# State products in pairs, a third one-pass block, one prefix scan and a new order, in a fused Mamba-2 and SiLU kernel on one core

## The chip, the core and the metric

The kernel runs on one NeuronCore of a Trainium2 chip. The core has five engines that run side by side, each with its own queue in program order: PE (matrix products; the loading of its stationary operand is shown apart, as PEld), DVE (vector operations), ACT (activations and copies), POOL (GpSimd) and SP, which here only issues DMAs. The metric is device time in microseconds, the median of several executions. One more execution was profiled; all durations of instructions below come from that one.

## What is computed

For each of 4 x 8 (batch, head) a state-space recurrence over 768 steps, in chunks, and behind it a SiLU layer over all tokens:

```python
# x (4,8,768,32)  a (4,8,768)  B, C (4,8,768,16), fp32
log_a = log(clip(a, 1e-6, 1));  cum = cumsum(log_a) within the chunk
y   = ((C @ B.T) * exp(cum_i - cum_j) * causal) @ x  +  (C @ state) * exp(cum)
state = exp(sum(log_a)) * state + (B * exp(cum_last - cum)).T @ x
# tokens (3072, 256) = y with the heads side by side
h = X @ w_in            # 256 -> 2048
out = (h * sigmoid(h)) @ w_out   # 2048 -> 256
```

All inputs and outputs are fp32.

## The kernel before

**Tiling.** The sequence work is cut into 12 units of 256 tokens of one batch (three units to a batch, numbered u = 0 to 11), each with four chunks of 64 steps. Two units make a pair (P = 0 to 5, 512 tokens), and the SiLU layer runs by pairs: W_in in 8 blocks of 256 columns (numbers 0 to 7), W_out in 8 blocks (8 to 15).

**Order.** Nothing is scheduled by a compiler. One text, SCHEDULE, lists some 1,300 tokens; each token calls one function, which issues its instructions. The order of tokens is the order of every engine's queue. SLOTS lists, in the order in which tiles are asked for, the buffer that each gets (pools of 49 tiles of 512 floats a partition, "s2k"; 12 of 1024, "r4k"; 7 of 1024, "raw"; 3 PSUM banks, "hp"). Two PSUM tiles of two banks each, ga and gb, serve the small products of the units and the first products of the SiLU layer in turn; one more bank, o_ps, serves the rest. Waits between engines follow from the tiles.

**Tokens of a unit u** (small products, with the array cut into tiles of 32 or 64 rows): `La` loads the decay of unit u, broadcast to all partitions, from a DRAM copy az; `E` (line 511) scans it to the matrix of decays; `Lp` loads the same values of a from a second DRAM copy, ac, and `P` (line 483) scans them to prefix products PFX; `Ln`, `Lt`, `Lx` load B, C and x; `T` transposes (line 524), `ce` scales C by head parity (545), `B` scales B by the decay (519, POOL), `C` scales C by PFX (550, POOL for most units). On PE: `gd` (function f_D0, line 570) makes each chunk's contribution to the state, `g0` (f_G0, 584) makes C.B for all chunks, `Y` (f_Y, 634 and 643) makes the output from the state and from the matrix M. On DVE `M` (599) multiplies g0's result by the decays, `S` (614) runs the state from chunk to chunk. ACT copies: `b` (593), `SM` (622), `y` (671), `xh` (678). `xh` and `x` split the unit's output into three parts, XK.

**Tokens of the SiLU layer.** fp32 products on PE take several passes per product; a product of fp32r operands takes one. So most of the layer is done with operands that are split into three parts, h, l and d, with one product for each part. `lw` loads a weight block, `u`, `v`, `w` and `W` turn it into a form whose parts can be cut exactly, `H` (line 322, ACT) cuts h, `lD` (326, DVE) makes l = h + w, `dD` (330, DVE) makes d = Z*h + l. For pair P and block i: `a` (line 799) does the h and l products of W_in, eight of 512 columns, `ax` (810, ACT) rescales in PSUM, `d` (799) adds four d products, `dg` (820, ACT) applies SiLU, `h`, `l`, `e` (826, 650, 836) split the result, and `q` (781) multiplies one half block by one half of W_out, three products. For pair 0, W_out is applied in full precision (`n1`, line 760), and W_in in full precision (`s`, line 696, one unit at a time, with `si` as SiLU) for blocks 0 to 5, and with `a` and `d` for blocks 6 and 7. `z` issues products with a zero tile whose result nobody reads (438: 512 columns; 440: six of 64 columns).

**a.** At the start i_a loads a for the first two units (`ia`), which PE transposes (`AT`); `ir` loads all of a, `AA,0` and `AA,1` clip it on POOL, `AD,4` writes az and `AD,0` to `AD,3` write ac, by POOL's DMA queue.

**Dead code that matters later.** Line 333 on has two functions that no token of before calls: w_part (an ACT copy of h, or of Z*h, into the tile for l or d) and w_more (a DMA issued by POOL that adds another tile to it), as `Wl`, `Wd` and `Wm`, `We`.

Of the kernel before, what the change touches and what calls it, by code (L numbers as in the profile page):

```python
# [30 lines left out]
w,9,2 dD,7 n1,1,1 ax,0,7 w,6,1 lw,10 s,0,2 w,6,2 v,15 u,10 w,15,2 d,0,7 si,0,2 W,11 lw,12 H,11 v,12 Lx,2,0,0 Lt,3,1,3,0
T,3,1 n1,0,0 v,13 n1,1,0 n1,6,1 La,2,1,0 dg,0,7 tq,2 La,2,0,0 E,2,1 W,15 w,10,0 n1,7,1 n1,15,1 n1,14,1 E,2,0 B,2 Lp,2,0
P,2 u,12 w,12,0 w,12,1 ce,2,0 Lt,3,0,2,0 g0,2 M,2,1 Lt,4,1,3,0 v,10 La,3,1,0 Lx,2,1,0 gd,2 n1,6,0 b,2,1 M,2,0 lw,14
n1,14,0 W,9 W,6 n1,2,0 w,13,2 Lt,3,0,1,0 n1,3,1 Lt,4,1,1,0 ce,3,1 H,5 Lx,3,0,0 H,9 b,2,0 S,2,0 S,2,1 S,2,2 ce,3,0 H,1
SM,2,1 n1,7,0 n1,15,0 C,2 u,14 SM,2,0 Y,2 La,3,0,0 E,3,0 W,13 v,14 si,1,4 w,10,2 y,2,0 Lt,4,1,2,0 H,6 E,3,1 Lt,3,0,3,0
T,3,0 Ln,3,0,1,0 Lx,3,1,0 Lp,3,0 P,3 n1,2,1 Ln,3,0,0,0 B,3 gd,3 w,12,2 W,12 Lt,4,0,0,0 lD,6 y,2,1 xh,2 g0,3 M,3,0 b,3,1
C,3 b,3,0 n1,10,1 n1,3,0 a,0,6 w,10,1 W,10 Lt,4,0,3,0 lD,0 S,3,0 S,3,1 M,3,1 dD,6 n1,11,0 H,13 S,3,2 Lp,4,0 w,14,0
Lt,4,1,0,0 w,14,1 Lx,4,1,0 ax,0,6 n1,10,0 x,2,1 H,15 SM,3,0 d,0,6 w,14,2 H,8 n1,5,0 La,4,1,0 n1,9,0 x,2,0 lD,5 La,4,0,0
E,4,0 Ln,4,0,1,0 dg,0,6 SM,3,1 Y,3 y,3,1 y,3,0 xh,3 lD,3 W,14 H,14 n1,13,0 n1,12,0 T,4,1 ce,4,0 n1,5,1 lD,9 n1,9,1 x,3,0
a,1,0 ax,1,0 n1,13,1 dD,5 Lt,4,0,2,0 x,3,1 n1,8,1 Lt,4,0,1,0 T,4,0 lD,1 ce,4,1 S,3,3 dD,0 d,1,0 P,4 C,4 n1,11,1 E,4,1  # L40
dg,1,0 lD,8 n1,12,1 dD,8 H,10 Lt,5,0,1,0 g0,4 Lx,4,0,0 Ln,4,0,0,0 B,4 H,4 gd,4 b,4,0 dD,1 M,4,1 b,4,1 S,4,0 S,4,1 S,4,2
SM,4,1 n1,4,0 M,4,0 Lt,5,1,1,0 SM,4,0 lD,4 Lt,5,1,0,0 lD,2 S,4,3 dD,2 h,1,0 dD,3 l,1,0 e,1,0 n1,8,0 n1,4,1 Vn,0 lD,10
Y,4 y,4,0 n1,0,1 y,4,1 a,1,1 xh,4 dD,10 H,12 lD,12 Vn,1 Lt,5,0,0,0 ax,1,1 a,1,2 ax,1,2 Lt,5,1,2,0 d,1,1 dg,1,1
Ln,5,0,0,0 Lt,5,1,3,0 T,5,1 La,5,1,0 o,0,0,2 q,1,0,0,1 La,6,1,0 ce,5,1 La,5,0,0 Ln,5,0,1,0 d,1,2 dg,1,2 h,1,2 ce,5,0
Lt,6,1,2,0 a,1,3 ax,1,3 q,1,0,1,1 a,1,4 ax,1,4 d,1,3 dg,1,3 Lp,5,0 q,1,0,1,0 E,5,1 E,5,0 B,5 o,0,1,2 lD,13 AD,2 lD,11
dD,4 Lx,5,0,0 l,1,2 e,1,2 d,1,4 dg,1,4 q,1,2,1,0 q,1,0,0,0 Lt,5,0,2,0 Lt,5,0,3,0 T,5,0 lD,15 dD,12 g0,5 x,4,1 Lx,5,1,0
Ln,6,0,0,0 gd,5 P,5 M,5,1 h,1,4 h,1,1 l,1,4 q,1,2,0,1 a,1,5 q,1,2,1,1 e,1,4 q,1,4,0,1 q,1,2,0,0 La,6,0,0 b,5,0 S,5,0
AD,3 Lt,6,1,1,0 q,1,4,0,0 b,5,1 ax,1,5 d,1,5 Ln,6,0,1,0 S,5,1 S,5,2 SM,5,0 M,5,0 SM,5,1 dD,13 Lt,6,1,3,0 x,4,0 q,1,4,1,1
q,1,4,1,0 C,5 dD,9 dg,1,5 h,1,5 Y,5 Lp,6,0 y,5,1 l,1,1 y,5,0 e,1,1 q,1,1,1,1 a,1,7 O,0,0,2,1,0 l,1,5 Lt,6,1,0,0
q,1,1,0,1 q,1,1,0,0 ax,1,7 e,1,5 d,1,7 Lt,6,0,0,0 xh,5 q,1,5,1,0 E,6,1 Lx,6,0,0 q,1,5,0,1 dg,1,7 Lt,6,0,3,0 T,6,1 ce,6,1  # L50
P,6 x,5,0 ce,6,0 Lt,6,0,2,0 Lt,6,0,1,0 T,6,0 q,1,5,0,0 E,6,0 h,1,7 C,6 g0,6 B,6 M,6,1 Lx,6,1,0 gd,6 b,6,0 Lt,7,1,2,0
h,1,3 q,1,1,1,0 S,6,0 M,6,0 dD,15 b,6,1 q,1,5,1,1 a,2,1 ax,2,1 S,6,1 S,6,2 SM,6,1 a,1,6 ax,1,6 l,1,7 e,1,7 q,1,7,0,0
q,1,7,0,1 d,1,6 dD,11 x,5,1 Lt,7,0,1,0 q,1,7,1,1 q,1,7,1,0 dg,1,6 d,2,1 l,1,3 e,1,3 lD,14 q,1,3,0,0 h,1,6 Lt,7,1,3,0
q,1,3,0,1 SM,6,0 l,1,6 dg,2,1 h,2,1 Y,6 La,7,1,0 y,6,0 e,1,6 Lt,7,1,0,0 Lx,7,1,0 S,6,3 Lt,7,1,1,0 T,7,1 ce,7,0 y,6,1
# [72 lines left out]
def kernel(  # L127
# [231 lines left out]
    def pz01(u):  # L359
        return held(f"pz{u}", [128, 4, Q + 1])  # L360
# [527 lines left out]
```

## Time and profile before

| | us |
|---|---|
| median of 3 runs | 333.38 (331.79 to 334.20) |
| the profiled execution: time | 333.58 |
| its span, first to last instruction | 331.8 |

| engine | busy us of 331.8 |
|---|---|
| PE | 321.9 |
| PE's weight loads | 244.0 |
| DVE | 250.8 |
| ACT | 204.9 |
| POOL | 48.6 |

The profile tells, for each engine, when each instruction began and ended, and what released it when its engine had been idle. Groups of instructions are named by the line of the kernel, the engine, the operation and the tiles (output <- inputs), with count, busy time, mean duration in ns, and the idle time just before them. The chain of work goes back from the last instruction, at each step to what released it. Durations of matmuls overlap, so the pace is read from the chain, not from the mean. 26.64 MB are moved by DMA, 80 GB/s on the mean; the ten loads of `pz` from ac carry 130 KB each.

### The profile page before, as it was taken

What the parts mean: (1) busy time and instruction counts of PE and PEld (TensorE: products, weight loads), DVE (VectorE), ACT (ScalarE), POOL (GpSimd) and SP (SyncE); (2) the same over time, 40 slices, a digit from 0 to 9 for tenths busy, and PEclk for the clock granted to TensorE, in tenths of its full rate; (3) what the DMA queues carried; (4) which work ended last, traced back from release to release, by engine and by line L of the source; (5) the groups of instructions that cost most, each with busy time, mean ns of one, the idle gap of its engine ahead of it and who ended that gap; (6) DMA issues with size and microseconds to landing.
All of it is one profiled execution on the core that took longest, in us unless ns stands there. A gap on an engine that the chain in (4) does not pass through costs nothing.

```text
span 331.8 us, 7522 instructions
## 1 busy us (share of the span) xinstructions
PE 321.9 (97%) x3078; PEld 244.0 (74%) x3078; DVE 250.8 (76%) x350; ACT 204.9 (62%) x309; POOL 48.6 (15%) x64
## 2 busy tenths in 40 slices
PE   6799999999999999999999999999999999999995
PEld 2478874455587878787887887877888787878884
DVE  4887899999999989698966678956486845453663
ACT  4669787644777565766566677726576367674811
POOL 2435565341111010010010100010000000000000
PEclk9769999999999999999999999999999999999999
DMA  5999478342253311245227241250003300031002
GB/s 173 218 276 256 173 202 197 63 94 34 69 117 69 73 48 21 53 109 123 29 38 152 73 89 30 38 111 2 2 9 70 58 2 0 2 54 18 2 0 63
DMA packets 93522, 26.64 MB, mean 80 GB/s; under 512 B 79840, under 2 KB 86752, under 8 KB 93488
## 3 DMA queue, kind: packets, MB, share of 16 engines
q1 hardware_dynamic: 90960, 25.71, 34.3%
q10 hardware_dynamic: 2352, 0.26, 0.6%
q8 instruction: 24, 0.39, 0.5%
q0 software_dynamic: 176, 0.20, 0.3%
q14 instruction: 10, 0.08, 0.1%
HBM read 22.81 MB, written 3.34 MB: 79 GB/s over the span
## 4 chain that ended last, share of the span: by engine, by line
PE 78%; DVE 12%; DMA 4%; ACT 2%; issue 1%; SPq 1%; POOL 1%; DVEq 0%; POOLq 0%
PE hp L781 27%; PE ga L799 15%; PE gb L799 15%; PE o_ps L781 5%; PE hp L696 5%; PE hp L760 3%; DVE ab L511 3%; PE ga L634 2%; PE ga L584 2%; PE ga L643 1%; DVE ab L599 1%; DMA bn<-in_B_dram 1%; DVE s2k L330 1%; DVE s2k L326 1%; DMA tbc<-in_C_dram 1%
## 5 line engine op out<-in xcount | busy, mean ns | idle before, releaser
L781 PE MATMUL hp<-r4k,s2k 128*128 128x512 f32 x400 | 109.5, 394 | 0.0
L781 PEld LDWEIGHTS hp<-r4k,s2k 128*128 128x128 f32 x400 | 74.0, 188 | 16.4 <-issue 0.5
L650 DVE SCALAR_TENSOR_TENSOR r4k<-r4k,r4k 128x1024 fp32r<-128x1024 f32 (+1 forms) x42 | 50.4, 1199 | 36.6 <-ACT r4k L826 28.9
L799 PE MATMUL ga<-raw,s2k 128*128 128x512 f32 x240 | 62.1, 394 | 0.0
L799 PE MATMUL gb<-raw,s2k 128*128 128x512 f32 x240 | 62.0, 393 | 0.1
L799 PEld LDWEIGHTS gb<-raw,s2k 128*128 128x128 f32 x240 | 44.5, 188 | 11.6 <-ACT gb L810 1.2
L799 PEld LDWEIGHTS ga<-raw,s2k 128*128 128x128 f32 x240 | 44.6, 188 | 11.3 <-ACT ga L810 1.2
L836 DVE SCALAR_TENSOR_TENSOR r4k<-r4k,r4k 128x1024 fp32r<-128x1024 f32 x40 | 48.7, 1222 | 4.9 <-PE o_ps L781 1.5
L826 ACT ACTIVATE r4k<-r4k 128x1024 fp32r<-128x1024 f32 x40 | 41.9, 1057 | 2.0 <-PE hp L781 0.5
L810 ACT ACTIVATE ga<-ga 128x1024 f32<-128x1024 f32 x21 | 21.2, 1009 | 20.5 <-PE ga L799 20.5
L820 ACT ACTIVATE r4k<-gb 128x1024 f32<-128x1024 f32 x21 | 21.5, 1025 | 15.6 <-PE gb L799 15.4
L810 ACT ACTIVATE gb<-gb 128x1024 f32<-128x1024 f32 x21 | 21.2, 1008 | 15.6 <-PE gb L799 15.6
L820 ACT ACTIVATE r4k<-ga 128x1024 f32<-128x1024 f32 x21 | 21.5, 1024 | 15.0 <-PE ga L799 13.8
L781 PE MATMUL o_ps<-r4k,s2k 128*128 128x512 f32 x80 | 30.7, 390 | 0.0
L760 PE MATMUL hp<-r4k,s2k 128*128 128x512 f32 x64 | 30.1, 602 | 0.0
L318 POOL TENSOR_TENSOR s2k<-s2k,s2k 128x512 uint32<-128x512 uint32 (+1 forms) x19 | 24.1, 1280 | 22.6 <-DVE s2k L310 13.7
L519 POOL TENSOR_TENSOR BT<-bn,ab 128x256 f32<-128x256 f32 x10 | 7.3, 730 | 120.3 <-DVE ab L511 87.5
L511 DVE TENSOR_TENSOR_SCAN ab<-ab,diag 128x512 f32<-128x512 f32 x20 | 24.8, 1246 | 0.0
L696 PE MATMUL hp<-r4k,s2k 128*128 128x256 f32 x96 | 22.9, 395 | 0.0
L696 PEld LDWEIGHTS hp<-r4k,s2k 128*128 128x128 f32 x96 | 18.7, 199 | 3.4 <-issue 0.4
L760 PEld LDWEIGHTS hp<-r4k,s2k 128*128 128x128 f32 x64 | 11.6, 189 | 10.8 <-issue 9.3
L599 DVE TENSOR_TENSOR ab<-gb,ab 128x512 f32<-128x512 f32 x12 | 8.2, 686 | 12.3 <-PE gb L584 7.4
(123 smaller groups left out, 390.9 us busy)
## 6 DMA issues: line engine op xcount, KB each, us to landing
ab<-az SPq DMA_DIRECT2D x20, 256.0 KB, 4.2
raw<-in_moe_w_in_dram SPq DMA_DIRECT2D x8, 512.0 KB, 4.1
raw<-in_moe_w_out_dram SPq DMA_DIRECT2D x8, 512.0 KB
out_dram<-r4k SPq DMA_DIRECT2D x44, 64.0 KB, 2.9
xt<-in_x_dram SPq DMA_DIRECT2D x20, 128.0 KB, 2.6
pz<-ac SPq DMA_DIRECT2D x10, 130.0 KB
bn<-in_B_dram SPq DMA_DIRECT2D x20, 64.0 KB, 3.6
tbc<-in_C_dram SPq DMA_DIRECT2D x36, 32.0 KB, 3.7
```

Of the source, the lines that this page charges most:

```text
L318: nc.gpsimd.tensor_tensor(out=u[:, :, fs], in0=u[:, :, fs], in1=v[:, :, fs], op=ALU.add)
L511: nc.vector.tensor_tensor_scan(out=o, data0=src, data1=diag.rearrange("p h t -> p (h t)"), initial=0.0, op0=ALU.mult, op1=ALU.add)
L599: nc.vector.tensor_tensor(out=o, in0=DP[u][w][:, :, 0:256].rearrange("p g (k x) -> p k g x", k=2), in1=o, op=ALU.mult)
L650: nc.vector.scalar_tensor_tensor(out=l, in0=f32(h), scalar=BACK, in1=y, op0=ALU.mult, op1=ALU.add)
L696: nc.tensor.matmul(out=hp[:, i], lhsT=WT[j][:, kc, 128 * i:128 * i + 128], rhs=XM()[:, 2 * kc:2 * kc + 2, u], start=(kc == 0), stop=(kc == ...
L760: nc.tensor.matmul(out=NP[m], lhsT=WT[8 + f // 2][:, f % 2, 128 * m:128 * m + 128], rhs=GT[0, f // 2][:, f % 2], start=(n == 1), stop=(n = ...
L781: nc.tensor.matmul(out=ACC[P, c], lhsT=WK[8 + i, p][:, k, 128 * m:128 * m + 128], rhs={"h": HT, "l": LT, "d": DT}[p][P, i][:, k], start=(n ...
L799: nc.tensor.matmul(out=o, lhsT=WK[j, q][:, kc, 128 * i:128 * i + 128], rhs=xs[:, 2 * kc:2 * kc + 2], start=(start and q == "h" and kc == 0 ...
L810: nc.scalar.activation(t, t, AF.Copy, scale=1.0 + Z)
L820: nc.scalar.activation(g, t, AF.Silu, scale=BACK)
L826: nc.scalar.activation(t, GT[G, i], AF.Copy, scale=-LESS * Z)
L836: nc.vector.scalar_tensor_tensor(out=DT[G, i], in0=f32(HT[G, i]), scalar=-1.0, in1=f32(LT[G, i]), op0=ALU.mult, op1=ALU.subtract)
```

## The change

It changes four things.

1. **Units 6 to 11 in pairs.** The tokens `Y,6` to `Y,11` become `YY,6`, `YY,8` and `YY,10`: f_Y does the state products of both units, then the products with M of both, into the two halves of ga and gb. So that the second unit of a pair can wait with its operands, its BT, CW and SM lie in a tile of the "raw" pool instead of the shared one, and its gd goes to other columns of ga. Before the first YY the order of gd and g0 is: gd,6 g0,6; gd,7; g0,7. Then gd,8; gd,9 g0,8; g0,9. Then g0,10 gd,11 gd,10; g0,11. (A semicolon stands where other products lie between.)
2. **Block 5 of pair 0** goes from `s` (two units) to `a,0,5`, `ax,0,5`, `d,0,5`, `dg,0,5`. `H,5`, `lD,5` and `dD,5` come earlier.
3. **One scan.** The ten `P` scans go. `AP` scans acp, all chunks and heads at once (48 partitions x 520), between `AA,1` and `AD,0`; so ac holds prefix products, and `Lp` loads them into PFX, two buffers in turn.
4. **A new order** of all tokens and slots. In it, W_out blocks 10 to 15 get l, and blocks 12 to 15 also d, by `Wl`/`Wm` and `Wd`/`We` instead of `lD` and `dD`. The large `z` go from 11 to 10, the groups of six small ones from 6 to 17; nine large and all 17 groups stand before the first `s`.

```diff
-cp cI c1 lw,4 ci z,1 z,1 z,1 z,1 ia,0 ct v,4 ia,1 z,1 z,1 z,0,6 z,1 cd ip,0,0 z,1 co u,4 ca A AT AU as,1,0 lw,0 ir,0 z,1
+ch ia,0 ca co cI cp ci z,0,6 z,0,6 z,0,6 ia,1 Lt,0,1,3,0 z,1 z,1 Ln,0,0,1,1 z,0,6 z,1 Ln,0,0,0,1 z,0,6 ip,0,0 c1 cd A AT
...
+q,2,1,1,1 h,2,2 g0,7 SM,6,0 q,2,1,0,1 q,2,0,1,1 M,7,1 q,2,0,0,1 M,7,0 SM,7,0 SM,7,1 YY,6 y,6,1 Lp,8,0 La,8,0,0 l,2,2
...
+PAIRS = (6, 8, 10)
...
-    one = const.tile([128, 4, Q + 1], FP32, name="one")
...
     def load_pz(u, q):
-        PZ[u] = keep("pz", [128, 4, Q + 1], loads)
+        PFX[u] = keep("pfx", [128, 4, Q + 1], loads2, u % 2)
...
-    def f_P(u):
-        PFX[u] = keep("pfx", [128, 4, Q + 1], loads)
-        nc.vector.tensor_tensor_scan(out=PFX[u].rearrange("p c t -> p (c t)"),
-                                     data0=PZ[u].rearrange("p c t -> p (c t)"),
-                                     data1=one.rearrange("p c t -> p (c t)"), initial=0.0,
+    def f_AP():
+        t = acp().rearrange("p h t -> p (h t)")
+        nc.vector.tensor_tensor_scan(out=t, data0=t, data1=one().rearrange("p h t -> p (h t)"), initial=0.0,
                                      op0=ALU.mult, op1=ALU.add)
...
+    def second(u, i):
+        return u - 1 in PAIRS and held(f"bc{u}", [128, 4, UT], key="raw")[:, i]
...
+        if not early and u - 1 in PAIRS:
+            d = [DP[u][0][:, c, 384:512] for c in range(2)]
...
-    def f_Y(u):
+    def f_Y(u, n=1):
         y = gy()
+        for v in range(u, u + n):
+            first = v % UPB == 0
+            st, cw, c0 = SM[v], CW[v], 128 * (v - u)
...
+        for v in range(u, u + n):
+            m, xc, c0 = M[v].rearrange("p k g (e t) -> p k (g e) t", e=2), xt[v], 128 * (v - u)
...
+            YO[v] = y, c0
```

The two functions that the new order calls and the old one did not:

```python
    def w_part(n, p):
        t = WK[n, p] = small(f"{p}{n}", [128, 2, WF], FR)
        nc.scalar.activation(t, f32(WK[n, "h"]), AF.Copy, scale=1.0 if p == "l" else Z)

    def w_more(n, p):
        other = WT[n] if p == "l" else f32(WK[n, "l"])
        nc.gpsimd.dma_start(out=f32(WK[n, p]).rearrange("p k f -> p (k f)"),
                            in_=other.rearrange("p k f -> p (k f)"), accum_op=ALU.add)
```

More of the change, by code (lines that the diff above doesn't have):

```diff
@@ L212, in f32 @@
         return t.bitcast(FP32)
-    bn, tbc, xt, E, M, BT, BH, CT, CE, CW, PFX, ST, SM, DP, BX, YS, PZ = ({} for _ in range(17))
+    bn, tbc, xt, E, M, BT, BH, CT, CE, CW, PFX, ST, SM, DP, BX, YS = ({} for _ in range(16))
     def at(u):
@@ L357, in acp, with one @@
         return held("acp", [NCH, H, Q + 1], key="r4k")
+    def one():
+        return held("one", [NCH, H, Q + 1], key="r4k")
     def pz01(u):
@@ L421, in c_one @@
     def c_one():
-        nc.gpsimd.memset(one, 0.0)
-        nc.gpsimd.memset(one[:, :, 0:1], 1.0)
+        nc.gpsimd.memset(one(), 0.0)
+        nc.gpsimd.memset(one()[:, :, 0:1], 1.0)
     def c_acp():
@@ L547, in f_C @@
     def f_C(u):
-        CW[u] = keep("cw", [128, UT], sc)
+        CW[u] = second(u, 1) if u - 1 in PAIRS else keep("cw", [128, UT], sc)
         engine = nc.vector if 0 < u < UPB else nc.gpsimd
@@ L619, in f_SM @@
         if u not in SM:
-            SM[u] = keep("sm", [128, 4, 64], sc)
+            if u - 1 in PAIRS:
+                SM[u] = second(u, 2).rearrange("p (t x) -> p t x", t=4)
+            else:
+                SM[u] = keep("sm", [128, 4, 64], sc)
         if True:
@@ new lines, in f_Y @@
+        for v in range(u, u + n):
+            first = v % UPB == 0
+            st, cw, c0 = SM[v], CW[v], 128 * (v - u)
+            for t in range(1 if first else 0, 4):
+                k, c = divmod(t, 2)
+                for g in range(4):
+                    w, q = divmod(g, 2)
+                    nc.tensor.matmul(out=y[w][64 * q:64 * q + 64, c, c0 + 64 * k:c0 + 64 * k + 64],
+                                     lhsT=st[32 * g:32 * g + 32, t], rhs=cw[32 * g:32 * g + 32, Q * t:Q * t + Q],
+                                     start=(v == u and (k == 0 or (first and t == 2))), stop=False,
+                                     tile_position=(32 * g, 64 * q), skip_group_check=True)
```

215 lines of the change are left out of this document (105 added, 110 removed), and 6 rows, old and new, of the table SLOTS.

## The prediction

> **What bounds the kernel now.** I read the page first: span, busy shares, the chain.
>
> ```profile
> span 331.8 us, 7522 instructions
> PE 321.9 (97%) x3078; PEld 244.0 (74%) x3078; DVE 250.8 (76%) x350; ACT 204.9 (62%) x309; POOL 48.6 (15%) x64
> PE 78%; DVE 12%; DMA 4%; ACT 2%; issue 1%; SPq 1%; POOL 1%; DVEq 0%; POOLq 0%
> ```
>
> A busy PE proves little, since its matmuls overlap; but 78% of the chain of work that ended last runs through PE too. Where the other 22% lie is seen by stretch (columns: busy time and count of PE, PE's weight loads, DVE, ACT, POOL, then granted clock, DMA share, GB/s):
>
> ```profile
> 10.00:20.00 10.00, 7.87 (x178) 5.53 (x174) 9.41 (x20) 5.70 (x14) 4.86 (x8) 0.60 0.98 219
> 20.00:30.00 10.00, 10.00 (x189) 7.99 (x189) 8.63 (x21) 7.77 (x17) 3.61 (x4) 0.89 1.06 341
> 60.00:110.00 50.00, 49.26 (x607) 32.02 (x607) 49.03 (x73) 31.66 (x54) 11.35 (x11) 1.00 0.37 77
> 110.00:320.00 210.00, 210.00 (x1863) 168.28 (x1863) 148.62 (x177) 130.06 (x172) 9.30 (x12) 1.00 0.23 46
> ```
>
> There are three stages: a start up to 20 us, in which PE's clock is granted at only 0.60 from 10 us on; then a stretch in which PE and DVE are both full (49.3 and 49.0 of 50 us); and from 110 us PE alone, with DVE at 148.6 of 210. How full PE really is, the chain shows between 206 and 222 us (start, length, what):
>
> ```profile
> 208.22 0.91 PE ga L799 x4
> 209.13 1.13 PE hp L781 x5
> ...
> 211.17 0.20 PE ga L634 x2
> 211.37 0.01 PE gb L634 x2
> 211.38 0.04 PE ga L634 x2
> ...
> 211.67 0.27 PE ga L643 x16
> 211.95 0.11 PE gb L643 x16
> ...
> 212.46 1.38 PE hp L781 x5
> ...
> 220.24 0.39 PE ga L570 x32
> 220.62 0.25 PE ga L584 x2
> ...
> 220.92 0.07 PE ga L584 x2
> ```
>
> A one-pass product of 512 columns costs 0.227 us (0.91 / 4, 1.13 / 5), back to back, and no other engine's piece stands between. The only loss is where the shape of the products changes: into Y's state products (L634) 0.20 where later pairs cost 0.04; from these into L643 0.27 where the next sixteen cost 0.11; out of them 1.38 where five cost 1.13. That is about 0.16, 0.16 and 0.25 us. For D0 (L570) and G0 (L584) likewise: 0.39 where two sixteens at 0.11 are 0.22, so 0.17; then 0.25 where 0.07 is the later step, so about 0.2.
>
> So behind the start the time is a sum of PE's work. What relieves DVE gains nothing by itself; what counts is PE's instructions, its changes of shape, the start, and new waits.
>
> **The change, part by part.**
>
> ```profile
> L483 DVE TENSOR_TENSOR_SCAN pfx<-pz,one 128x260 f32<-128x260 f32 x10 | 7.2, 716 | 2.5 <-DMA pz<-ac 2.5
> L326 DVE TENSOR_TENSOR s2k<-s2k,s2k 128x512 fp32r<-128x512 f32 x16 | 13.2, 836 | 0.6 <-ACT s2k L322 0.6
> L330 DVE SCALAR_TENSOR_TENSOR s2k<-s2k,s2k 128x512 fp32r<-128x512 f32 x16 | 12.2, 771 | 0.1
> L322 ACT ACTIVATE s2k<-s2k 128x512 fp32r<-128x512 f32 x16 | 9.8, 626 | 0.0
> L599 DVE TENSOR_TENSOR ab<-gb,ab 128x512 f32<-128x512 f32 x12 | 8.2, 686 | 12.3 <-PE gb L584 7.4
> ac<-r4k POOLq DMA_DIRECT2D x4, 24.4 KB, 3.8
> L467 POOL DMA_DIRECT2D ac<-r4k x4: 562/708/804, 42.3 to 99.2; - x4
> 29.11 8.84 PE hp L696 x40
> ```
>
> *The third one-pass block.* Two s of block 5 go, 8 recorded products each: 16 x 0.221 (8.84 / 40) = 3.54 us. In come a,0,5 and d,0,5, 12 x 0.227 = 2.72. PE gains 0.82 us. Block 5's split (lD 0.84, dD 0.77 on DVE) moves forward and is hidden by the s and Y that stand on PE before a,0,5; without them the block would be late by these 1.6 us.
>
> *One scan.* Ten scans of 0.716 leave DVE; one of 520 elements comes, by its length about 1.4. DVE gains 5.8 us and loses a wait of 2.5 us for pz: 0 on the path, since PE is what is full. The new scan stands between AA,1 and the DMAs that write ac, so Lp and C wait for it; E waits on az, which it doesn't touch.
>
> *W_out blocks 10 to 15.* Six lD and four dD leave DVE (6 x 0.836 + 4 x 0.771 = 8.1 us). Ten ACT copies come (at 0.626, 6.3 us; ACT then has about 212 of 332), and ten accumulating DMAs on POOL's queue, which this trace does not show. The nearest rows are ac's DMAs: 0.71 us of POOL and 3.8 us to landing, for a tenth of the data. Queued behind them on POOL are B,6, B,7 and C,5 onwards. The tightest is block 14: We,14 waits for Wm,14's landing, both stand behind B,7 and We,15, and q,1,6,0,0 needs the result. That is 3 x 0.71 + 2L behind B,7, with L a landing: 9.7 us at 3.8. PE has from B,7 to there four a (8 x 0.227 = 1.81 each), three d (0.91), eight q (0.68) and one gd (about 0.4): 15.8 us. That is the cover; the price is 0, and 2L - 13.7 from L = 6.8 on. From the other side: were DVE's 8.1 us on the path they would be a gain, but DVE's share above excludes that from 110 us on. I take 0.
>
> *Pairs.* Three Y runs go: 3 x (0.16 + 0.16 + 0.25) = 1.7 us. But D0 and G0 of the second unit no longer stand together: in pairs 6 and 8, gd and g0 of the odd unit have other products between them, one exit and entry more for one inner change less (about 0.2 each); pair 10 saves a change. Net 1.3 (0 to 1.7). Against it: PE stops in front of YY until DVE has M of the second unit. Between g0,9 and YY,8, and between g0,11 and YY,10, stand two q, 1.36 us; two M take 2 x 0.69 = 1.37 and a hand-over at both ends. I put 0.3 us on these two and 0.2 on YY,6, which has three q: 0.8 us, from 0 to 1.4 (one M each). The Y of before had ten products and more there.
>
> *The start*, rows of SP, DVE and PE in time, then groups of the first 24 us:
>
> ```profile
> 0.81 0.45 SPq L288 DMA_DIRECT2D raw<-in_moe_w_in_dram  x1
> 4.54 0.21 DVE L445 TENSOR_SCALAR s2k<-s2k 32x128 f32<-32x128 f32 x1 [1.61 <-DMA s2k<-in_a_dram]
> 5.62 0.24 PE L450 MATMUL o_ps<-ident,s2k 32*128 32x32 f32 x1
> 17.13 0.37 PE L634 MATMUL ga<-cw,sm 32*64 32x64 f32 x2 [0.56 <-DVE ab L599]
> 19.99 3.03 PE L696 MATMUL hp<-r4k,s2k 128*128 128x256 f32 x8
> L438 PE MATMUL o_ps<-s2k 128*128 128x512 bf16 x11 | 4.7, 536 | 2.2 <-DVE s2k L385 1.9 <-DVE s2k L454 0.3
> L440 PE MATMUL o_ps<-s2k 128*64 128x64 bf16 x30 | 2.0, 217 | 0.0
> L519 POOL TENSOR_TENSOR BT<-s2k,ab 128x128 f32<-128x128 f32 x4 | 1.9, 468 | 7.9 <-DMA s2k<-in_B_dram 7.8
> ```
>
> Now a's DMAs are the first of SP, not behind the weight block that takes 0.45 of issue: DVE's first step (4.54) comes 0.5 earlier. The transposition of a (5.62) stood behind eight large and six small dummy products, 8 x 0.43 + 6 x 0.067 = 3.8 us; now behind three large and thirty small, 3.3. B is issued from ACT at once, and POOL waited 7.8 us for it. So Y,0 and s,0,0 move forward by 0.5 at least if nothing else holds them, and by up to 2 where B's wait counted. Against it: 102 small dummies instead of 30, two large fewer, before s,0,0: +72 x 0.067 - 2 x 0.43 = 4.0 us, if PE never waits there. It does wait there now (0.56 for M). I take 1.0 us earlier, from 2 earlier to 2 later (half of those dummies).
>
> The clock: the first eight s products took 3.03 us, not 8 x 0.221 = 1.77, and the window at 10 us had 0.60 granted. More dummies keep PE busier; I take half of that 1.26, 0.6. [...] One z,1 now stands behind s,0,0: +0.2.
>
> The sum, against the profiled execution's 333.58 us (span 331.8 and 1.8 around it; the median of the runs is 333.38): -0.82 - 1.3 + 0.8 - 1.0 - 0.6 + 0.2 = -2.7, so 330.9; against the median 330.7. I say **330.8 us**.
>
> **Rivals.**
> 1. *The start brings nothing.* The dummies delay the first product as much as the loads bring it forward, and the clock stays shut: 333.58 - 0.82 - 1.3 + 0.8 + 0.2 = 332.5, and 334.5 with the start 2 us later. For it: PE executes dummies in order, 102 of them. Against: PE waited for DVE there anyway.
> 2. *All of it comes.* Start 2 us earlier, clock open (1.3), no wait at YY: 333.58 - 0.82 - 1.3 - 2 - 1.3 + 0.2 = 328.4. For it: 14 us less DVE before 110 us, where DVE was as full as PE. Against: PE had hardly a wait there that could go.
> 3. *Slower: the accumulating DMAs.* They are ten times larger than ac's and read their target before they write it. If a landing takes 11 us, q,1,6,0,0 is 2 x 11 - 13.7 = 8.3 us late, and PE, being in order, with it: 339.2. It decides from L = 9.9: there 2L - 13.7 = 6.1 eats the 2.7 and adds 1%. Against: ac's DMAs took 0.71 us of POOL while DVE was full.
> [...]
> 4. *The pairs save nothing*, since runs of small products go only from 25 to 24: 332.2.
>
> **How the numbers follow.** Forecast 0.45 (329.3 to 332), rival 1 0.2, rival 2 0.15, rival 3 and any order that starves PE for 6 us 0.16, rival 4 0.04. 1% is about what a measurement of this kernel can tell from no change: 3.3 us, so faster is below 330.0 and slower above 336.7. Faster: all of rival 2 and some 0.2 of the forecast's lower part, 0.35. Slower: 0.16. Within: 0.49. The range takes in the likelier cases from rival 2 to the first half of rival 3: 328.0 to 336.5.
>
> **What would show it.** Of the profile after: L696 x80 and L799 with twelve more; the first s at 18 to 20 us, and its eight products near 1.8 us if the clock is open; DVE at about 237 us; the chain almost all PE from there, with three YY runs entered once each, and idle of at most 0.5 us on PE before them, put down to M. I'm wrong if PE shows waits of over 1 us behind 25 us: for a weight part (L781 for a POOL DMA, rival 3), for B,7's load, or for DVE at a YY; or if the first s starts after 21 us.

## The result, and the profile after

| | before | after |
|---|---|---|
| median, us | 333.64 (4 runs, 331.79 to 334.20) | 338.46 (4 runs, 336.45 to 338.59) |
| profiled execution: time, span | 333.58, 331.8 | 336.45, 334.7 |
| end of the last one-pass product in it | 327.00 | 329.32 |

After to before is 1.0151, with a 95% interval of 1.0108 to 1.0195: slower by 4.8 us, outside the predicted range. The profiled execution is the fastest of the four (the other three have spans of 335.4, 335.8 and 335.9), while those of shift_minus and large_for_small below, at 343.4 us each, are the slowest of theirs.

From the page of after: span, busy time, the DMA queues of engine programs, and the chain.

```profile
span 334.7 us, 7659 instructions
PE 322.7 (96%) x3139; PEld 247.2 (74%) x3139; DVE 242.5 (72%) x331; ACT 211.4 (63%) x319; POOL 55.0 (16%) x74
q8 instruction: 24, 0.39, 0.5%
PE 81%; DVE 6%; DMA 5%; SPq 2%; issue 2%; ACT 2%; POOL 0%; DVEq 0%; POOLq 0%; ACTq 0%
```

DVE lost 8.3 us, where the prediction had 13.9 (to about 237; the one scan alone took 2.31 us instead of 1.4), and the chain runs through PE even more than before. By stretch (columns as in the prediction):

```profile
10.00:20.00 10.00, 7.07 (x190) 4.80 (x188) 9.82 (x20) 6.01 (x13) 4.71 (x7) 1.00 0.99 196
20.00:30.00 10.00, 10.00 (x243) 8.04 (x220) 7.37 (x17) 6.78 (x16) 3.20 (x3) 0.83 1.04 287
60.00:110.00 50.00, 48.52 (x656) 31.47 (x656) 44.34 (x67) 35.84 (x66) 17.19 (x19) 1.00 0.70 132
110.00:320.00 210.00, 209.08 (x1864) 168.55 (x1863) 142.24 (x166) 130.47 (x173) 11.96 (x16) 1.00 0.28 51
```

PE is idle 0.7 us more between 60 and 110, 0.9 more behind, 0.8 more between 10 and 20. The view of waits of PE behind 16 us (total, times, longest) names what it stood for:

```profile
PE ga L663 <- issue: 2.2, 1, 2.2
PE o_ps L801 <- DVE r4k L856: 0.8, 1, 0.8
PE ga L580 <- DMA xt<-in_x_dram: 0.5, 1, 0.5
PE ga L819 <- DVE raw L670: 0.5, 1, 0.5
```

The largest is "issue": PE waited for nothing that the profile shows. On PE's timeline it stands in the middle of Y,0, between two products of one call:

```profile
17.29 0.32 PE L663 MATMUL ga<-ab,s2k 64*32 64x64 f32 x9
19.75 0.26 PE L663 MATMUL ga<-ab,s2k 64*32 64x64 f32 x4 [2.15 <-issue]
...
21.77 2.99 PE L716 MATMUL hp<-r4k,s2k 128*128 128x256 f32 x8
```

Before had no such line. The first `s` (L716 here, L696 before) begins at 21.77 instead of 19.99, and its eight products take 2.99 us, as cold as before.

From the end of the products ahead of the first s to the last one-pass product before took 306.8 us (20.20 to 327.00), after 307.4 (21.97 to 329.32), although products of 0.82 us and three changes of shape are gone: PE's new waits, 1.1 us at 102 and 0.7 at 127 the longest, ate the saving. (This counts what PE's pace lost; as idle time alone the view has 0.8 and 0.5.) Behind that product the span has 5.4 us instead of 4.8. So the 2.9 us between the two profiled executions are 1.8 at the start, 0.6 in between and 0.6 at the end.

### The profile page after: what moved, and what is told of

It is laid out like the page before. It is cut to its first block, busy times and chain, and to the rows that moved or that the text cites. A ratio compares the mean times of both kernels' runs of the same rounds, so it can differ in the third digit from the quotient of the medians.

```text
span 334.7 us, 7659 instructions
## 1 busy us (share of the span) xinstructions
PE 322.7 (96%) x3139; PEld 247.2 (74%) x3139; DVE 242.5 (72%) x331; ACT 211.4 (63%) x319; POOL 55.0 (16%) x74
## 4 chain that ended last, share of the span: by engine, by line
PE 81%; DVE 6%; DMA 5%; SPq 2%; issue 2%; ACT 2%; POOL 0%; DVEq 0%; POOLq 0%; ACTq 0%
PE hp L801 25%; PE ga L819 16%; PE gb L819 16%; PE hp L780 7%; PE hp L716 5%; PE o_ps L801 5%; PE ga L594 1%; PE ga L663 1%; DVE ab L513 1%; DMA xt<-in_x_dram 1%; DMA ab<-az 1%; DMA s2k<-in_C_dram 1%; PE ga L652 1%; DMA tbc<-in_B_dram 1%; PE gb L663 1%
## 5 line engine op out<-in xcount | busy, mean ns | idle before, releaser
L801 PE MATMUL hp<-r4k,s2k 128*128 128x512 f32 x400 | 109.5, 393 | 0.0
L801 PEld LDWEIGHTS hp<-r4k,s2k 128*128 128x128 f32 x400 | 74.1, 188 | 16.5 <-issue 0.9
L819 PE MATMUL ga<-raw,s2k 128*128 128x512 f32 x240 | 62.9, 396 | 0.5 <-DVE raw L670 0.5
L830 ACT ACTIVATE gb<-gb 128x1024 f32<-128x1024 f32 x22 | 22.2, 1008 | 18.0 <-PE gb L819 18.0
L801 PE MATMUL o_ps<-r4k,s2k 128*128 128x512 f32 x80 | 30.9, 392 | 0.8 <-DVE r4k L856 0.8
L780 PE MATMUL hp<-r4k,s2k 128*128 128x512 f32 x64 | 30.4, 602 | 0.0
L840 ACT ACTIVATE r4k<-gb 128x1024 f32<-128x1024 f32 x22 | 22.5, 1025 | 10.2 <-PE gb L819 8.7
L319 POOL TENSOR_TENSOR s2k<-s2k,s2k 128x512 uint32<-128x512 uint32 (+1 forms) x19 | 23.2, 1233 | 28.4 <-DVE s2k L311 16.7
L716 PE MATMUL hp<-r4k,s2k 128*128 128x256 f32 x80 | 19.7, 398 | 0.1
L780 PEld LDWEIGHTS hp<-r4k,s2k 128*128 128x128 f32 x64 | 11.6, 189 | 9.8 <-issue 8.6
L716 PEld LDWEIGHTS hp<-r4k,s2k 128*128 128x128 f32 x80 | 15.8, 202 | 3.7 <-issue 1.5
L801 PEld LDWEIGHTS o_ps<-r4k,s2k 128*128 128x128 f32 x80 | 15.0, 188 | 4.5 <-DVE r4k L856 1.2
L527 POOL TENSOR_TENSOR BT<-bn,ab 128x256 f32<-128x256 f32 x7 | 5.1, 733 | 66.8 <-DVE ab L513 48.9
```

The costliest lines, as they stand in the source:

```text
L319: nc.gpsimd.tensor_tensor(out=u[:, :, fs], in0=u[:, :, fs], in1=v[:, :, fs], op=ALU.add)
L716: nc.tensor.matmul(out=hp[:, i], lhsT=WT[j][:, kc, 128 * i:128 * i + 128], rhs=XM()[:, 2 * kc:2 * kc + 2, u], start=(kc == 0), stop=(kc == ...
L780: nc.tensor.matmul(out=NP[m], lhsT=WT[8 + f // 2][:, f % 2, 128 * m:128 * m + 128], rhs=GT[0, f // 2][:, f % 2], start=(n == 1), stop=(n = ...
L801: nc.tensor.matmul(out=ACC[P, c], lhsT=WK[8 + i, p][:, k, 128 * m:128 * m + 128], rhs={"h": HT, "l": LT, "d": DT}[p][P, i][:, k], start=(n ...
L819: nc.tensor.matmul(out=o, lhsT=WK[j, q][:, kc, 128 * i:128 * i + 128], rhs=xs[:, 2 * kc:2 * kc + 2], start=(start and q == "h" and kc == 0 ...
L830: nc.scalar.activation(t, t, AF.Copy, scale=1.0 + Z)
```

## The experiments

**What stands where.** PE's program is loaded while it runs: q8 brings it, 24 times 16 KB (0.39 MB). I took such a block for 256 instructions, 128 products with their weight loads: the stands found below lie 256 apart, and in after each of the first 24 borders that these places give has one load, which begins between 3.9 us before and 5.7 us behind the first product there. I numbered PE's instructions in the program (products, weight loads and waits; 6,346 in after) and looked up each stand, a gap on PE put down to "issue", of over 0.5 us behind 16 us. The lengths of stands in the text run from the start of one product to the start of the next, 0.2 to 0.3 us more than the idle time in the views.

Theory A came first: 72 more dummies are 144 more instructions, and the stock of instructions is used up while the weights fill the DMA engines. Against it theory S (order and loads), and, for the waits at 102 and 127, theory B: the accumulating DMAs hold up other loads.

**1. Twelve groups of small dummies fewer** (fewer_small).

```diff
-lw,5 v,5 cP u,5 ab,1,1 z,0,6 z,0,6 E,0,0 B,0,0 z,0,6 Lt,0,1,2,0
+lw,5 v,5 cP u,5 ab,1,1 E,0,0 B,0,0 Lt,0,1,2,0
...
```

> The changed kernel without the last 12 of its 17 groups of six small dummy products (11 of the 12 stand ahead of Y,0), nothing else moved. Theory A, the stock of PE's instructions: each group is 12 instructions for 0.40 us of work, the first block of further code reaches PE only at 16.9 us, and PE stands 2.15 us in front of Y,0's last products because its stock is used up. Then the stand falls below 0.5 us, the first entry of eight s products ends near 20.2 us instead of 21.97, and the time falls by 1.8 us, to about 336.7. Theory S, order and loads: PE stands there for something that has to do with the loads and not with its own code; the stand stays near 2 us, the first s within 0.5 us of 21.97, and the time within 0.6 us of 338.5.

Measured: 337.24 us, 1.0099 (1.0062 to 1.0137). The stand at Y,0 is gone, as A says, though the first s begins only 0.9 us earlier (20.89), not 1.8. And 0.9 us stand in Y,1, and 2.1 us in the middle of YY,6, at 155.65, where nothing was changed and no weight is loaded. A explains at most the start.

**2. A large dummy for each of these twelve groups** (large_for_small).

```diff
-z,0,6
+z,1
```

> The same 12 groups are each replaced by one large dummy product: 0.43 us of work for 0.40, but 2 instructions instead of 12. Theory A (stock of instructions): as without them, the stand of 2.15 us falls below 0.5 us, and the time is near 336.7; PE stays as busy as it was, so the first eight s products may run with an open clock and save another 1 us. Theory S (order and loads) and also the reading that the dummies' mere time is the cost: no change, 338.5 within 0.6, stand of 2 us where it was.

Measured: 340.89 us, 1.0238 (1.0187 to 1.0290); both theories miss. In the profile stand 2.1, 1.7 and 1.7 us in the three YYs, 1.7 in Y,1.

**3. W_out's splits on DVE again** (vector_split).

```diff
-Wl,10
...
-Wm,10
+lD,10
...
-Wd,12
...
-We,12
+dD,12
...
```

> The changed kernel with all W_out splits on DVE again: lD and dD stand where Wm and We stood, Wl and Wd are gone. Ten accumulating DMAs of 256 KB and ten ACT copies go, DVE gets 8.1 us. Theory B, the accumulating DMAs: they delay loads (DVE waited 1.97 us in front of the scan of E,6, PE then 1.09 us at 102.65 and 0.72 at 127.09). Then both of these waits go and the time falls by about 1.8 us, to 336.7, and more if these DMAs also cause the 1 us by which the time exceeds the span more than before. Rival D, DVE is full up to 110 us: its 8.1 us come onto the path in part, and the time rises to 340 to 344; the waits at 102 and 127 grow or stay.

Measured: 337.61 us, 1.0140 (1.0111 to 1.0170). The wait at 102 falls to 0.2, the one at 127 becomes one for POOL (0.8), and new stands of 2.3 us in G0,1 and 1.3 in YY,10 appear. The time lies between B's and D's. Not clean: its program is 8 instructions shorter.

**4. The kernel before with twelve groups more** (before_plus_small). Some of them overwrite o_ps while it holds B of unit 0 transposed, so y of unit 0 is another; the instructions are the same.

```diff
-T,0,1 C,0 Ln,1,0,0,0 ir,3 Lx,0,0,0 tp,0
+T,0,1 z,0,6 C,0 z,0,6 Ln,1,0,0,0 ir,3 Lx,0,0,0 tp,0 z,0,6
...
```

> The kernel before with 12 more groups of six small dummies, spread over the preparations ahead of Y,0. Theory A (stock of instructions): a stand of about 2 us put down to nothing appears in front of s,0,0 or a little earlier, and the time rises by about 2 us, to 335.6. Theory S (order and loads): no such stand; the dummies fill PE's waits for data, of 4.8 us at most 1 us stays, 333.6 to 334.6.

Measured: 337.91 us, 1.0142 (1.0099 to 1.0186). Stands of 1.9 us in G0,1 and 2.8 in an s, both later than A had it, and none behind 35 us. It has single Ys.

The places of the stands, from these five traces and the next (number in PE's program, and distance from 193 + 256 k):

```
after               17.60 us  2.37   453 (+4)
fewer_small         27.26     0.93   707 (+2)   155.65 2.08 3523 (+2)   257.74 0.53 5570 (+1)
large_for_small     26.93     1.70   703 (-2)   159.41 2.05 3519 (-2)   210.83 1.71 4543 (-2)   263.46 1.69 5566 (-3)
vector_split        17.62     2.36   449 (0)     24.13 2.31  705 (0)    256.57 1.26 5568 (-1)
before_plus_small   23.62     1.89   707 (+2)    31.15 2.79  962 (+1)
shift_minus         19.69     0.53   453 (+4)    26.47 2.34  709 (+4)
                   159.32     1.06  3525 (+4)   208.33 2.09 4549 (+4)   261.27 1.98 5572 (+3)
```

All lie within 4 instructions of 193 + 256 k (the trace of large_for_small lacks three products, so its numbers are up to 6 low). That is theory F: the borders of the program's blocks. In YY,8 of shift_minus PE entered a block at 206.56; the next was loaded from 207.64 to 208.82; PE had used up the first at 208.33 and went on at 210.19, 3.6 us after it had entered. In YY,10 it was 3.6 as well, in YY,6 2.7. While the weights load, the load of a block mostly begins 2 to 6 us after the entry (3.8, 5.7, 3.8 and 3.8 us at the first four borders of after), and the next block is open only after 6 to 8.6 us (6.6 in after, which entered a block at 13.1 and went on at 19.75).

The expectations below put a YY at 192 instructions in 1.7 us, which is wrong: it counts the calls, and in the trace an fp32 call stands as two products (64 at L780 of after for the 32 calls of `n1`; the fp32r calls at L801 as one, 480 for 480). There a YY has 184 to 192 products with as many weight loads, 368 to 384 instructions in 2.4 to 2.5 us; a single Y has 176 to 192 in 1.3 to 1.4 us. So a Y is shorter than a block, and a YY is longer: it may hold two borders, and the block between them lasts 1.8 us where 3.6 are needed.

**5. The shift alone, both ways** (shift_minus, shift_plus). Five groups of dummies, ahead of a's transposition where PE waits anyway: 60 instructions fewer, 60 more.

```diff
-ch ia,0 ca co cI cp ci z,0,6 z,0,6 z,0,6 ia,1 Lt,0,1,3,0
+ch ia,0 ca co cI cp ci ia,1 Lt,0,1,3,0
...
```

> The changed kernel without its first five groups of six small dummies (they stand ahead of a's transposition, where PE waits for a anyway): PE's program is 60 instructions shorter, all else is the same. Theory F, borders of code blocks: PE's program comes in blocks of 256 instructions; the next block is asked for when PE enters one and can be used some 3.4 us later (7 us while the weights load); in every trace so far PE's stands put down to nothing lie at instruction 193 + 256 k. A YY is 192 instructions in about 1.7 us. By these lengths the shift of 60 puts a border into each of the three YYs: stands of about 1.6, 1.9 and 1.8 us near 157, 208 and 260 us, and 2.8 us at Y,0; the time rises by about 3 us, to 341. Rival: the stands have to do with the order, the loads or the dummies' time: with fewer dummies the time stays or falls, 337 to 338.5, and no new stand appears at the YYs.

```diff
-c1 cd A AT
+c1 cd z,0,6 z,0,6 z,0,6 z,0,6 z,0,6 A AT
```

> The reverse: five more groups of six small dummies ahead of a's transposition, 60 instructions more. Theory F (borders of code blocks): no border lies within a YY, the stands at Y,0 fall to 0.4 us and grow behind 28 us to about 2.8; the time is 337 to 338, and the 1.1 us by which time less span was larger in the changed kernel (its program ended nine instructions behind a border) goes. Rival (dummies' time, order, loads): 60 dummies more are no gain anywhere; the time is 338.5 to 340.5, the 2.4 us at Y,0 stay.

Measured: 339.39 us, 1.0219 (1.0169 to 1.0270), and 332.92 us, 1.0020 (0.9991 to 1.0050). In the first the YYs hold the three stands foretold (1.1, 2.1 and 2.0 us for 1.6, 1.9 and 1.8); the 2.8 of Y,0 came as 0.5 there and 2.3 in Y,1. The times that F gave, 341 and 337 to 338, are missed: the sign is right, but shift_plus gains over 4 us more than foretold. The chain of waits of shift_minus through YY,8 (start, length, what):

```profile
208.15 0.18 PE gb L664 x11
208.33 1.86 issue
210.19 0.24 PE gb L664
```

and PE's waits behind 100 us, first of shift_minus, then all there are of shift_plus:

```profile
PE gb L664 <- issue: 3.6, 2, 1.9
PE ga L581 <- DMA xt<-in_x_dram: 1.1, 1, 1.1
PE ga L664 <- issue: 0.8, 1, 0.8
PE ga L759 <- DVE r4k L747: 0.5, 1, 0.5
```

```profile
PE ga L759 <- DVE r4k L747: 0.5, 1, 0.5
```

The same products in the same order but for 60 dummies, 120 instructions: 6.5 us. The rival would have it the other way round. A stand cost more than its length where the clock fell behind it. In the profiled execution of shift_minus 0.50 was granted behind YY,10, where nine products of 512 columns took 3.3 us (they take 2.0 at 0.227 each):

```profile
250.00:264.30 14.30, 12.51 (x264) 9.94 (x263) 9.64 (x12) 8.33 (x13) 0.00 (x0) 1.00 0.20 31
264.40:267.70 3.30, 3.30 (x9) 2.59 (x8) 1.29 (x2) 1.83 (x4) 0.00 (x0) 0.50 0.02 5
```

Laid side by side product by product, the profiled executions of shift_minus and shift_plus drift apart by 2.3 us ahead of 50 us, 1.4 at 127, 1.1 at YY,6, 2.1 at YY,8 and 3.6 at YY,10, the closed clock with it: 10.5 in all, where the medians differ by 6.5. In shift_plus the waits at 102 and 127 are gone too, with all ten accumulating DMAs in place: B is not needed for them.

**6. The same shift by fewer dummies** (fewer_shifted). One group of the 17 is left.

> The changed kernel with only the first of the 17 groups of small dummies: against the run with 12 fewer (337.24, of which 2.1 us are a stand in YY,6 and 0.7 behind YY,10) it has 48 instructions fewer. Theory F (borders of code blocks): the borders move out of the three YYs; no stand over 0.5 us at any YY, one of about 2.7 us near 27 us; the time falls by 2.8 us, to 334.4. Rival: those stands do not depend on where the code lies; the time stays at 337 within 1.

Measured: 332.70 us, 0.9989 (0.9965 to 1.0012). No stand at a YY, 1.6 us in Y,1. The saving against fewer_small, 4.5 us, is more than the 2.8 foretold. Of the 3.4 us between the two profiled executions 2.1 arise at YY,6 and 0.7 at the stand at 257.7; the rest is not traced. Here YY,8 in the chain:

```profile
202.65 0.15 PE gb L663 x9
202.80 0.16 PE ga L663 x8
202.97 0.20 PE gb L663 x12
203.17 0.66 PE hp L801 x2
```

**7. The same, and the splits on DVE** (fewer_shifted_vector; edit of 3).

> As the run before, and W_out's splits on DVE again (no accumulating DMAs). Theory F with B (accumulating DMAs delay loads): the wait of 1.1 us at 102 us goes as it did in the run with only this change; the time is 333 to 334, no longer slower than the kernel before by more than 0.3%. Rival D (DVE is full): 1 to 2 us more than the run without this, 335.5 to 336.5.

Measured: 334.24 us, 1.0049 (1.0025 to 1.0073), 1.5 more than without. With the borders harmless, the accumulating DMAs are a gain: without them PE waits 0.85 us at 126.6 for POOL's B,7, 0.3 at 103 for DVE. B falls; D, DVE being full, holds in part.

**8. The YYs cut in two**, on shift_minus (minus_split) and on fewer_shifted (fewer_shifted_split); what is computed stays.

```diff
-YY,6 y,6,1 Lp,8,0 La,8,0,0 l,2,2 e,2,2 q,2,2,1,1 q,2,2,0,0
+Ya,6 y,6,1 Lp,8,0 La,8,0,0 l,2,2 e,2,2 q,2,2,1,1 q,2,2,0,0 Yb,6
```

> The kernel with 60 instructions fewer (339.39 us; stands of 1.06, 2.09 and 1.98 us within the three YYs), with each YY cut in two: all products of the first unit, two q, all products of the second. What is computed and the number of PE's instructions stay. Theory F (borders of code blocks): a block that holds a YY now lasts some 1.9 us longer, two q (1.36) and one more change of shape (0.57), so the block behind it has arrived: the three stands fall from 5.1 to 0.5 us in all, the three more changes of shape cost 1.7; the time is 336 to 337. Rival: the stands do not come from the length of the run of small products; then the time rises by the 1.7 us, to 341.

> The same cut of the three YYs in the kernel with only one group of small dummies (332.70 us), where no border of a block falls into a YY. Here only the price of the changes of shape is left: if a run of small products costs 0.57 us to enter and leave, as the prediction has it, the time rises by 1.7 us, to 334.4. Rival (the pairs save nothing): 332.7 within 0.5.

Measured: 337.20 us, 1.0121 (1.0090 to 1.0151): the cut *saves* 2.2 us where borders lie in the YYs, and all three stands are gone. And 335.61 us, 1.0086 (1.0051 to 1.0120): it *costs* 2.9 where none does. Both have a new wait of 0.8 at `a,2,1`, ga being read by ACT for longer (minus_split):

```profile
162.58 1.20 PE L820 MATMUL ga<-raw,s2k 128*128 128x512 f32 x4 [0.82 <-ACT ys L692]
```

Product by product, the profiled fewer_shifted_split falls behind fewer_shifted by 1.5, 0.5 and 1.0 us at the three YYs, and by another 1.1 at the start, which the cut doesn't touch. Less that wait of 0.8, the three changes of shape cost 2.2, foretold 1.7. So the pairs save about what the prediction said, and are what makes the borders dear.

**9. Three small moves on fewer_shifted** (best_try).

```diff
-n1,14,0 a,1,0 n1,9,1
+n1,14,0 n1,9,1 a,1,0
...
-ab,0,1 lw,5 v,5
+ab,0,1 Lx,0,0,0 Lx,0,1,0 lw,5 v,5
...
-Vt,5,1,0 Vt,5,1,1 ot,5,1,0 or,5,1,0 os,5,1,0,0 Vt,5,1,2 Vt,5,1,3 ot,5,1,1
+Vt,5,1,2 Vt,5,1,3 Vt,5,1,0 Vt,5,1,1 ot,5,1,1 ot,5,1,0 or,5,1,0 os,5,1,0,0
```

> The kernel with one group of small dummies, and three small moves that leave the places of the code's borders as they are: the product n1,9,1 goes ahead of a,1,0 (PE waits there 0.72 us for x of unit 3), the loads of x for unit 0 go ahead of the first weight block (PE waits 3.8 us for them in front of D,0, but the chain over C and ACT is only some 0.5 us shorter), and the last output half is written in the order of the kernel before (its last store landed 0.5 us sooner). Theory F: -0.7 -0.5 -0.5, 331.0 us, and a stand of about 1.6 us stays near 26 us. If the start is bound by the first code blocks, 331.5 to 332.

Measured: 333.31 us, 1.0020 (0.9991 to 1.0048): no gain. The wait for x at 77 went, but g0,0 now waits 1.8 us for ce (C's loads now stand behind x's), and the stand in Y,1 is 2.7 us instead of 1.6.

**10. Control: the kernel before with the five groups of shift_plus** (before_shifted).

> Control: the kernel before with the same five groups of small dummies ahead of a's transposition that took the changed kernel from 338.46 to 332.92. Theory F: the kernel before has no run of small products long enough to use up a block behind 35 us, so the place of the borders matters only at the start: 332.5 to 334. Rival: the dummies themselves helped (a warmer PE, an earlier start): then this one gains too, and falls to 331 or below.

Measured: 332.83 us, 1.0004 (0.9977 to 1.0031). The dummies that gave the changed kernel 5.5 us give this one nothing.

**11. Where the 5.5 us lie: the program's end, the later borders** (longer_end, later_shift). Six products more behind the last; and the five groups at 45 us (there they overwrite o_ps while it holds B and C of unit 2 transposed, which changes y of unit 2).

```diff
-ot,5,1,1 or,5,1,1 os,5,1,1,1
+ot,5,1,1 or,5,1,1 os,5,1,1,1 zi,6
```

> The changed kernel with six small products behind its last one, 24 instructions of PE more, so that the program no longer ends nine instructions behind the border of a code block. Nothing ahead of them is touched. Theory F2: in the changed kernel PE asks for one more block when it passes that border, and the program can't end before it has come; this is the 1.1 us by which its time less its span was 2.8 to 2.9 in three of four runs and 1.7 in nearly all runs of the other kernels. Then time less span is 1.7 in every run here, and the time falls by 1.0, to 337.4. Rival: the 1.1 us come from something else of the changed kernel (its accumulating DMAs, its last stores): time less span stays near 2.9, the time at 338.5.

```diff
-w,10,2 w,10,1 W,10 n1,5,0
+w,10,2 w,10,1 W,10 z,0,6 z,0,6 z,0,6 z,0,6 z,0,6 n1,5,0
```

> The changed kernel with the five more groups of six small dummies not at the start but at 45 us, ahead of n1,5,0, where PE is full (60 instructions, 30 products, about 1 us). Behind 45 us the borders lie as in the kernel with the five groups at the start (332.92 us); ahead of it as in the changed kernel. Theory F with the start as the larger part: the stand of 2.4 us at Y,0 and the later first s stay, the end's 1.1 us goes, the stand in YY,8 (0.3) goes, 1 us comes for the dummies: 338, five more than with the dummies at the start. If the five us came from the later borders instead, 334 to 335. Open beside it: whether PE's waits at 102 and 127 us (1.09 and 0.72) go, which went in the kernel with the dummies at the start.

Measured: 336.02 us, 1.0090 (1.0064 to 1.0116), and 335.54 us, 1.0083 (1.0055 to 1.0112). Time less span is 1.7 in all four runs of either; in after it was 2.9, 2.8 and 2.7 in the three runs that weren't profiled:

```
after         338.34-335.4  338.58-335.8  338.59-335.9   profiled: 336.45-334.7
longer_end    336.40-334.7  336.00-334.3  336.04-334.3   profiled: 335.52-333.8
```

The end was worth more than foretold, 2.4 us, since the span fell too. That is half of what after lost. later_shift has it too and gets back only 0.5 more, with 1 us of dummies in it; the other 2.6 us to shift_plus are due to the start (and the dummies): product by product the two profiled executions are 2.9 us apart by 60 us and 2.7 at the end. But later_shift, whose program is that of after up to 45 us, has no stand at Y,0. There x came 1.0 us later (PE waited 1.7 us for it instead of 0.7), the clock was granted at 0.50 between 15 and 20 us instead of 1.00, PE reached the border after the block had come, and the first s began at 22.25, later than with the stand. The waits at 102 and 127: longer_end has the first (1.1) and not the second, later_shift neither.

**12. One wait less on shift_plus** (plus_and_swap: the swap of n1,9,1 and a,1,0).

> The kernel with five more groups of small dummies at the start (332.92 us), and n1,9,1 ahead of a,1,0, where PE waits 0.72 us for x of unit 3. No border moves. Theory F: that wait goes and nothing comes for it, 332.2 us. Rival: DVE, which is late there, is late at the next place, 332.9.

Measured: 334.03 us, 1.0007 (0.9981 to 1.0034). The wait for x went; the time did not move by anything that this can measure.

No version beats the kernel before. The change without stands in the YYs (fewer_shifted; 1.6 us stay in Y,1) equals it, and is 1.7% faster than the change as it was made (332.70 to 338.46).

## Why the prediction was wrong

*The start* is the step that failed: "102 small dummies instead of 30 ... +4.0 us if PE never waits there. It does wait there now ... I take 1.0 us earlier." It priced the dummies as time on PE, and took PE's waits as cover. The first s came 1.8 us later instead, past the 21 us that the prediction had named as a sign of being wrong. A dummy of 0.067 us costs two instructions whatever it waits beside; with 144 more of them ahead, PE was at the border of its second block, instruction 449, at 17.6 us, and that block's load had begun only at 16.94. Four traces have this same start: in after, vector_split and longer_end PE stood there (2.15, 2.13 and 2.52 us of idle time), and the first s began at 21.77, 21.27 and 21.94. In later_shift PE was late without it (x later, clock closed: 22.25), so the stand is not the whole of it. With 60 instructions more ahead, in shift_plus, there is no stand at Y,0, and the first s began at 20.44. The forecast had no term for the loads of the program, 24 of 16 KB in the traces of before and of after.

*Pairs*, -1.3: right in itself (2.2 for three cuts, against 1.7 before what D0 and G0 give back). What was missing is its price: a run of small products twice as long is longer than a block of the program, and can use one up before the next is there. That was on no line of the sum, and no rival had it. In after's profiled run the borders happen to lie almost clear of the YYs (0.3 us at YY,8); 60 instructions less, and the stands in them add up to 5.1 us.

*The clock*, -0.6: it was open with the dummies, 1.00 granted from 10 to 20 us instead of 0.60; then came the stand, and the eight s took 2.99 us. In fewer_shifted, which has no stand there, 1.89 (1.00 granted from 20 to 30 us, 0.66 from 10 to 20):

```profile
20.03 1.89 PE L716 MATMUL hp<-r4k,s2k 128*128 128x256 f32 x8
```

That half of the 1.26 us would be saved was the author's estimate: in after next to nothing was (2.99 for 3.03), in fewer_shifted nearly all (1.89 for 1.77). The granted clock of before is 1.00 from 5.2 to 11.9 us, 0.50 from 12.0 to 22.1 and 1.00 from 22.3 to 40, that of after 1.00 from 10.4 to 20.5, 0.50 from 20.6 to 23.9 and 1.00 from 24 to 40; so in both some 2.2 us of the eight s, which began at 19.99 and at 21.77, ran at 0.50. What decided it is not settled: fewer_shifted has 16 groups of dummies less, vector_split the same stand and yet 1.00 from 10 to 40 us and 1.89 for the eight s, and before took 3.03 without a stand.

*Waits at the YYs*, +0.8: mis-sized. In no run does the view of waits put 0.2 us or more at a YY down to M.

*The third block*, -0.82: L716 x80 as foretold. *The scan*, 0: no wait of PE is put down to it, though it took 2.31 us and not 1.4.

*Accumulating DMAs*, 0: the landings kept under the 6.8 us from which they were to cost. The line of the ten of them in after:

```profile
L340 POOL DMA_DIRECT2D s2k<-s2k x10: 852/907/1181, 78.0 to 138.5; - x10
...
DMA to landing us min/median/max: 3.3/4.4/6.0
```

Issue and landing were bounded well from ac's rows (0.91 for 0.71, 4.4 for 3.8). But the other reason for 0, that DVE's share "excludes that from 110 us on", was wrong: with DVE's 8.1 us back (fewer_shifted_vector) the time is 1.5 us longer, by the waits at 103 and 126.6 us.

*What lies around the span*, taken as 1.8: 1.1 more in three of four runs. The program ends nine instructions behind a border (6,337), and longer_end, which moves only the end away from it, has none of the 1.1; what is waited for there no trace shows. vector_split, which ends one behind it, has 2.4 and 2.8 in two of four runs; all kernels whose programs end elsewhere have 1.7 or 1.8.

*Rival 1* had the start about right in size (2 us later, clock shut: 334.5), though by the dummies' time; the waits at 102 and 127 and the 1.1 around the span are not in it.

*Rival 3*, the only one beyond the range, gave 339.2 for another reason; its landings never came near 9.9 us. That the time is close to it is chance.

Open: the two waits that make up 1.8 us of the slowdown, that is why PE waits at 102 us for DVE (which stood 1.97 us in front of the scan of E,6, whose load was issued at 93.1) and at 127 for x of unit 7. Their lines were touched by no experiment, and they came and went with shifts of a microsecond. That the load of a block comes late at the start (in after it begins 3.8 to 5.7 us behind the first four borders, with a DMA share of 0.99 from 10 to 20 us and 1.04 from 20 to 30, and 0.2 to 1.4 behind most later ones) because the weights fill the DMA engines fits every trace, but no run took those loads away. Nor is it settled why the longer end also shortens the span, by 1.3 us.

## What to carry to other kernels

An instruction had a price of its own in these runs: count those of PE between two borders of 256, and compare the time that they take with the time in which a block arrives (here 2.7 to 3.6 us, 6 to 8.6 while the weights load). Dummies, and longer runs of small products, spend that stock. Where a profile shows "issue" inside one call's products, look for the border first, and shift the program by some dozens of instructions before explaining anything else: two kernels that differ in 60 dummies, and by them in the place of the borders, differed by 6.5 us, more than any part of this change was worth.

## What was not expected of the hardware

- The next block is loaded only about when PE enters one: in after, behind 60 us, its load begins between 3.9 us before and 1.4 us after the first product of the block before it (2.0 to 3.9 before it at five borders, each behind products of 512 columns at 0.22 to 0.24 us; why, no trace shows) and takes 0.9 to 1.5 us. Where PE stood behind 100 us, it went on 1.4 to 1.5 us after the load had ended.
- Programs that end nine or one instructions behind a border (after, vector_split) took 0.7 to 1.2 us longer around the span in five of eight runs.
- Behind stands of 1.5 to 2.2 us of idle time the granted clock was 0.50 for some 3.3 us: in after behind Y,0 (20.6 to 23.9), in shift_minus behind Y,1 and YY,10, in large_for_small behind Y,1 and YY,6. In vector_split, behind 2.13 us, it stayed at 1.00.
